# Fourth product of a fused attention and two-layer chain: a third pair of token tiles in seven block products, weights converted by contraction block

## The chip, the cores and the metric

The kernel runs on one core of one Trainium2 chip. The metric is the device time of one execution in microseconds (us). Engines are named as in the profile: PE is TensorE (matmuls), PEld its weight loads, ACT is ScalarE, DVE is VectorE, POOL is GpSimd, SP is SyncE, which issues the transfers here.

## The reference

```
attn = softmax(mask(q @ k^T / 8)) @ v            # 2 x 12 heads, 448 tokens, 64 wide
x    = attn as rows                               # 896 tokens x 768
h    = x @ moe_w_in;  g = h * sigmoid(h);  x = g @ moe_w_out      # 768 -> 2048 -> 768
h    = x @ w_in                                   # third product, 768 -> 1024
e    = exp(h - max(h));  solu = h * e / sum(e)
ln   = (solu - mean) / sqrt(var + 1e-6) * g_ln
out  = ln @ w_out                                 # fourth product, 1024 -> 768
```

The inputs are 64-bit floats in memory; the kernel converts the weights itself. Every product is made as three fp32r matmuls on a high and a low part of each operand (high x high, high x low, low x high).

## The kernel before, in words

The change touches the last two products. The 896 tokens are seven tiles of 128 (t = 0 to 6).

**Third product.** `gemm3(t)` makes 36 matmuls of 512 columns into a two-bank PSUM tile `h`; even tiles use the pool `psh0`, odd ones `psh1`, so tile t + 2 overwrites tile t. `chain(t)` takes the maximum on VectorE (L840, "reduce"), the exponential on ScalarE (L841, into the SBUF tile `e`) and, as the inner function `share`, the sums and the product on VectorE (L844 to L847). `scaled(t)` squares on ScalarE into `h` (L855, the last use of `h`), subtracts the mean from `e` (L856, ScalarE) and takes `rstd` from a small VectorE operation (L857) and a power on GpSimd (L858).

**Conversion of the fourth weight.** It comes in 16 chunks of 128 x 384 64-bit numbers. `feed4`, called through `fill` between the pieces of `chain`, works on a few of them at a time: ScalarE scales the upper words (`conv_a`, L259), VectorE puts the words together (`sign_low` L264, `shift_w` L276, `rest_high` L271), then `high4` (ScalarE, L772) and `low4` (VectorE, L777) give the high and low part of gain x weight. The 16 blocks are `b11`, `b21`, `b12`, `b22` (row half, column half), each of four contraction chunks k. Before, the chunks come block by block.

**Fourth product.** `turn(t)` transposes a tile: 16 small matmuls from `e` to the PSUM tile `tp`. Its tiles come from the list `turns`, first only `pst` (one buffer), later also `pstb`; each call takes the first pool of the list and moves it to the end. ScalarE and VectorE read `tp` into operands (high, L879; low, L883). One product is `product`: four k by three matmuls of 384 columns.

- `whole(t, n)` makes one column half of one tile in two products, four products a tile.
- `pair4(g)` makes tiles a = 2g + 1 and b = 2g + 2 together in seven products in place of eight, by seven sums of operands: "11", "12", "s4", "s2", "s3", "s1", "22" on the left with b11, b21, b22 and the sums of weights `t2`, `t3`, `t1`, `t4` on the right. `pre(g, n)`, n = 0 to 5, makes the left operands of a pair: n = 0 turns tile b, n = 1 turns tile a, n = 2 makes "s4", n = 3 to 5 make "s2", "s3", "s1", with a subtraction of 128 x 512 on GpSimd each.
- `sums4(k)` makes the sums of weights of chunk k (before: four scalings on ScalarE, L1020, four subtractions on GpSimd, L1022 to L1025); `split_t` splits them into high (ScalarE, L1030) and low (VectorE, L1031).

The order is written by hand. After every product `after()` runs the steps of a table, by number of the product. Before: tiles 0, 1 and 2 by `whole` (12 products), then `pair4(1)` and `pair4(2)` (14), 26 in all. The sums of weights are made at products 0 to 11. Engines work through their instructions in program order.

The output of a product lies in a PSUM bank of the pool `gm` (two buffers), for pairs in turn with `psq`, which lies where `psh0` was.

Of the kernel before, what the change touches and what calls it, by code (L numbers as in the profile page):

```python
# [8 lines left out]
F32 = mybir.dt.float32  # L9
F32R = mybir.dt.float32r  # L10
# [12 lines left out]
KD = DM // 128  # L23
# [63 lines left out]
def fused(ctx, tc, qk, vv, w1, w2, w3, w4, gl, out):  # L87
# [32 lines left out]
    with tc.manual_schedule():  # L120
# [153 lines left out]
        def shift_w(n, c):  # L274
            low = wraw[n, c][:, :, 0]
            nc.vector.tensor_scalar(low, low, 29, None, ALU.logical_shift_right)  # L276

        def top_bits(n, c):
            x = wx[n, c] = psw.tile([128, 512], F32, name="pw", tag="pw")[:, :CH]
            r = wraw[n, c]  # L280
            if n == 1 or n == 2 and c % 2 and c < HEAD + 4 * PARTS:
# [9 lines left out]
        def fresh(where):  # L291
            return where.tile([128, CH], F32, name="wx", tag="wx")
# [468 lines left out]
        aop[0, 1], aop[0, 2] = [pair_of(n, lambda m: spare[m]) for n in range(2)]  # L761

        def quad(m):
            n, k = divmod(m, KF2)
            return f"{k // K2 + 1}{n + 1}", k % K2, gain[:, k:k + 1]

        quads = {}

        def high4(m):
            z, k, g = quad(m)  # L770
# [2 lines left out]

        def low4(m):
            z, k, g = quad(m)
            h, l = split[4, z]
            nc.vector.scalar_tensor_tensor(l[:, k], quads[z, k], g, h[:, k].bitcast(F32), ALU.mult, ALU.subtract)  # L777
            ready.add((4, m))

        def feed4(between=lambda: None):  # L780
            m = fed[0]
            fed[0] += 1
            old = [order[pend.pop(0)][1] for _ in range(min(2, len(pend)) if len(pend) >= XS else min(1, len(pend)))]
            for c in old[:-1]:
                high4(c)
                low4(c)
            for c in old[-1:]:
                high4(c)
            if m < len(order):
                sign_low(*order[m], fresh(x4))  # L790
                if m + 1 < len(order):
                    shift_w(*order[m + 1])
                rest_high(*order[m])
                pend.append(m)
            between()
            for c in old[-1:]:
# [55 lines left out]
        def scaled(t):  # L852
            e, p3 = es4[t], hps[t].rearrange("p n (m q) -> p (n m) q", m=K2)
            col = lambda m: marks[t][:, m:m + 1]
            nc.scalar.activation(p3, e, AF.Square, bias=col(5), accum_out=col(6))  # L855
            nc.scalar.activation(e, e, AF.Identity, bias=col(5))  # L856
            nc.vector.tensor_scalar(col(7), col(6), 1.0 / DF2, 1e-6, ALU.mult, ALU.add)  # L857
            nc.gpsimd.tensor_tensor(col(9), col(7), mhalf, ALU.pow)  # L858
            rstd[t] = col(9)

# [120 lines left out]
        for t in range(NT):  # L981
            gemm3(t)
            if t == 0:
                fill()
            if t == NT - 2:
                turn(0)

            def first(between):
                if t == NT - 2:
                    take(0)  # L990
                fill(between)

            if t < NT - 1:
                chain(t, first, fill)
                scaled(t)
        areas = [token_rows(q, k)[:, :512] for q in "hl" for k in range(KD)] + spare[4:]
        places = {(1, 1): 0, (1, 2): 1, (2, 1): 2, (2, 2): 3}
        for g, at in ((1, (4, 5, 6, 7, 8, 9, None)), (2, (0, 1, 2, 3, None, 4, 5))):
            for z, n in zip(("11", "12", "s4", "s2", "s3", "s1", "22"), at):
                places[g, z] = n  # L1000
        for z, n in places.items():
            if n is not None:
                aop[z] = pair_of(n, lambda m: areas[m])
        aop[1, "22"], aop[2, "s3"] = aop[0, 1], aop[0, 2]

        def arrive(t):
            turn(t)
            take(t)

        arrive(1)  # L1010
        while pend:
            fill()
        w3p.release()
        t4p = pool("t4", side="right")
        for z in ("t2", "t3", "t1", "t4"):
            split[4, z] = [t4p.tile([128, K2, CH], F32R, name=f"{z}{p}", tag=f"{z}{p}") for p in "hl"]

        def sums4(k):
            for n, z in enumerate(QUADS):
                nc.scalar.activation(quads[z, k], quads[z, k], AF.Copy, scale=gain[:, k + K2 * (n // 2):k + K2 * (n // 2) + 1])  # L1020
            b11, b12, b21, b22 = [quads[z, k] for z in QUADS]
            nc.gpsimd.tensor_tensor(b11, b12, b11, ALU.subtract)  # L1022
            nc.gpsimd.tensor_tensor(b12, b12, b22, ALU.subtract)
            nc.gpsimd.tensor_tensor(b22, b22, b11, ALU.subtract)
            nc.gpsimd.tensor_tensor(b21, b21, b22, ALU.subtract)  # L1025

        def split_t(k):
            for z, q in (("t2", "22"), ("t3", "12"), ("t1", "11"), ("t4", "21")):
                h, l = split[4, z]
                nc.scalar.activation(h[:, k], quads[q, k], AF.Copy)  # L1030
                nc.vector.tensor_tensor(l[:, k], quads[q, k], h[:, k].bitcast(F32), ALU.subtract)  # L1031

        def pre(g, n):
            a, b = 2 * g + 1, 2 * g + 2
            s1, s3, s2, s4 = [rows(half(*at)) for at in ((b, 1), (b, 0), (a, 0), (a, 1))]
            if n == 0:
                turn(b)
# [22 lines left out]
        steps = {1: [lambda: sums4(1)], 2: [lambda: arrive(2)], 3: [lambda: split_t(0)], 4: [lambda: sums4(2)],  # L1060
                 5: [lambda: pre(1, 0)], 6: [lambda: sums4(3)], 7: [lambda: pre(1, 1)],
                 8: [lambda: scaled(NT - 1), lambda: split_t(1)], 9: [lambda: pre(1, 2)], 10: [lambda: split_t(2)],
                 11: [lambda: pre(1, 3), lambda: split_t(3)], 12: [lambda: pre(1, 4)], 13: [lambda: pre(1, 5)],
                 14: [lambda: pre(2, 0)], 15: [lambda: pre(2, 1)], 16: [lambda: pre(2, 2)],
                 17: [lambda: pre(2, 3), lambda: pre(2, 4)], 18: [lambda: pre(2, 5)]}
        at = iter(range(26))

        def after():
            for step in steps.get(next(at), ()):
                step()  # L1070

        sums4(0)
# [12 lines left out]
        turns[0].release()  # L1085
# [51 lines left out]
```

## Time and profile before

| what | value |
| --- | --- |
| median of 3 runs | 397.21 us (396.82 to 398.51) |
| profiled execution | 397.12 us |
| its span, first to last instruction | 395.2 us |
| PE busy | 387.5 us, 98% |
| DVE, ACT, POOL busy | 73%, 71%, 48% |
| mean granted TensorE clock | 1.000 |

Between the time of the profiled execution and its span lie 1.9 us that no engine shows. A time in a row counts from the start of the span. "x16" is the number of instructions that a row merges; the bracket at a row's end is the idle time before it and what ended it.

### The profile page before, as it was taken

The page shows a single profiled execution, that of the slowest core. Times are in us where ns is not written, and L with a number is a line of the kernel's source. Part 1 is how long each engine was busy: PE and PEld are TensorE (multiplying, and loading weights), DVE is VectorE, ACT ScalarE, POOL GpSimd, SP SyncE. Part 2 cuts the span into 40 slices and gives each one's busy share as a digit, 9 for nine tenths or more (in the row PEclk, how much of TensorE's full clock was granted, in tenths as well). Part 3 has the DMA queues.
Part 4 walks back from the last instruction along what each step waited for, and adds up shares of the span by engine and source line. Part 5 has one row for each costly group of instructions (what it writes and reads, how often), then busy time and mean ns, then how long its engine had stood idle before and what let it go on. Part 6 is the DMA issues. An engine that isn't in the chain of part 4 may idle for free.

```text
span 395.2 us, 8157 instructions
## 1 busy us (share of the span) xinstructions
PE 387.5 (98%) x2914; PEld 364.0 (92%) x2914; DVE 290.3 (73%) x681; ACT 279.7 (71%) x655; POOL 188.6 (48%) x236
## 2 busy tenths in 40 slices
PE   8799999999999999999999999999999999999996
PEld 5677888999999999999999999999988888999995
DVE  3999999477665755677566577776999996667943
ACT  5999998756474655775666787786767874998530
POOL 3898897324372563638566345554001000595450
PEclk9999999999999999999999999999999999999999
DMA  7964202244434343446343667787024310011121
GB/s 235 399 213 139 101 7 77 81 127 153 127 116 119 121 119 120 117 124 202 89 152 120 191 179 230 238 245 224 14 80 121 98 62 2 20 41 41 41 81 60
DMA packets 20152, 49.68 MB, mean 126 GB/s; under 512 B 2320, under 2 KB 4880, under 8 KB 20112
## 3 DMA queue, kind: packets, MB, share of 16 engines
q1 hardware_dynamic: 20112, 49.16, 39.7%
q8 instruction: 23, 0.38, 0.4%
q14 instruction: 17, 0.14, 0.1%
HBM read 46.40 MB, written 2.75 MB: 124 GB/s over the span
## 4 chain that ended last, share of the span: by engine, by line
PE 92%; DVE 4%; ACT 3%; issue 0%
PE h L397 8%; PE h L396 8%; PE h L395 8%; PE h L824 5%; PE h L825 5%; PE h L826 5%; PE ps L904 5%; PE h L555 4%; PE h L557 4%; PE h L556 4%; PE ps L906 4%; PE ps L905 4%; PE x L229 4%; PE x L164 3%; ACT e L175 3%; PE x L202 2%
## 5 line engine op out<-in xcount | busy, mean ns | idle before, releaser
L259 ACT ACTIVATE wr<-wr 128x384 f32<-128x384 f32 x92 | 54.3, 591 | 10.4 <-DMA wr<-w_in 10.2
L396 PE MATMUL h<-l,wh 128*128 128x448 f32 x174 | 61.3, 352 | 0.0
L395 PE MATMUL h<-h,wh 128*128 128x448 f32 x174 | 61.3, 352 | 0.0
L397 PE MATMUL h<-h,wl 128*128 128x448 f32 x174 | 61.3, 352 | 0.0
L289 DVE SCALAR_TENSOR_TENSOR pw<-wr,pw 128x384 uint32<-128x384 uint32 x78 | 43.5, 557 | 13.3 <-ACT pw L285 13.2
L188 POOL TENSOR_TENSOR e<-e,st 128x64 f32<-128x64 f32 (+6 forms) x76 | 45.5, 633 | 11.4 <-DVE st L170 6.9
L414 POOL TENSOR_TENSOR gl<-sg,gh 128x448 fp32r<-128x448 f32 x29 | 32.7, 1145 | 36.9 <-ACT sg L412 36.9
L175 ACT ACTIVATE e<-e,st 128x256 f32<-128x256 f32 (+6 forms) x84 | 41.8, 507 | 4.2 <-DVE st L170 4.1
L326 DVE TENSOR_TENSOR wl<-pw,wh 128x384 fp32r<-128x384 f32 x30 | 16.7, 557 | 32.5 <-ACT wh L322 31.8
L322 ACT ACTIVATE wh<-pw 128x384 fp32r<-128x384 f32 x30 | 14.8, 493 | 36.1 <-PE h L396 27.5
L170 DVE CUSTOM_DVE_ANT_0 e<-x,mask 128x448 f32<-128x448 f32 (+6 forms) x84 | 30.5, 414 | 5.4 <-PE x L164 5.4
L858 POOL TENSOR_TENSOR s<-s,mhalf 128x1 f32<-128x1 f32 x7 | 4.2, 594 | 61.3 <-DVE s L857 61.3
L326 POOL TENSOR_TENSOR wl<-wx,wh 128x384 fp32r<-128x384 f32 x21 | 21.2, 1008 | 25.5 <-ACT wh L322 25.4
L395 PEld LDWEIGHTS h<-h,wh 128*128 128x128 f32 x174 | 32.9, 189 | 0.1
L397 PEld LDWEIGHTS h<-h,wl 128*128 128x128 f32 x174 | 32.9, 189 | 0.0
L396 PEld LDWEIGHTS h<-l,wh 128*128 128x128 f32 x174 | 32.9, 189 | 0.0
L824 PE MATMUL h<-w3h,h 128*128 128x512 f32 x84 | 31.9, 380 | 0.0
L825 PE MATMUL h<-w3l,h 128*128 128x512 f32 x84 | 31.9, 379 | 0.0
L826 PE MATMUL h<-w3h,l 128*128 128x512 f32 x84 | 31.8, 379 | 0.0
L555 PE MATMUL h<-gh,wh 128*128 128x448 f32 x90 | 31.7, 352 | 0.0
L557 PE MATMUL h<-gh,wl 128*128 128x448 f32 x90 | 31.7, 352 | 0.0
L556 PE MATMUL h<-gl,wh 128*128 128x448 f32 x90 | 31.7, 352 | 0.0
(294 smaller groups left out, 1104.1 us busy)
## 6 DMA issues: line engine op xcount, KB each, us to landing
wr<-w_in SPq DMA_DIRECT2D x96, 384.0 KB, 3.2
qk<-qk_in SPq DMA_DIRECT2D x11, 448.0 KB, 5.5
v<-vv_in SPq DMA_DIRECT2D x12, 256.0 KB, 6.6
out<-o SPq DMA_DIRECT2D x14, 192.0 KB, 1.9
qk<-qk_in SPq DMA_DIRECT2D x2, 128.0 KB, 2.8
qk<-qk_in SPq DMA_DIRECT2D x1, 192.0 KB, 3.4
gain<-gl_in SPq DMA_DIRECT2D x1, 4.0 KB, 3.9
```

The source lines that it names most:

```text
L175: nc.scalar.activation(ep(p, u), ep(p, u), AF.Exp, bias=st[p % 4][:, u:u + 1], scale=-1.0, accum_out=st[p % 4][:, 8 + u:9 + u])
L188: eng.tensor_tensor(ep(p, u), ep(p, u), r.to_broadcast([128, wide(u)]), ALU.mult)
L259: nc.scalar.activation(high, high, AF.Copy, scale=DOWN)
L395: nc.tensor.matmul(ps[:, :S], wh, rh, start=turn == 0 and k % NB == 0, stop=False)
L396: nc.tensor.matmul(ps[:, :S], wh, rl, start=False, stop=False)
L397: nc.tensor.matmul(ps[:, :S], wl, rh, start=False, stop=turn == 1 and k % NB == NB - 1)
L555: nc.tensor.matmul(ps[:, :S], wh, rh, start=f == CF[0], stop=False)
L556: nc.tensor.matmul(ps[:, :S], wh, rl, start=False, stop=False)
L557: nc.tensor.matmul(ps[:, :S], wl, rh, start=False, stop=f == CF[-1])
L824: nc.tensor.matmul(ps[:, n], yh[k][:, at], wh, start=k == 0, stop=False)
L825: nc.tensor.matmul(ps[:, n], yh[k][:, at], wl, start=False, stop=False)
L826: nc.tensor.matmul(ps[:, n], yl[k][:, at], wh, start=False, stop=k == KD - 1)
```

## The change

- Tiles 1 and 2 become a third pair, `pair4(0)`, ahead of the others: four products of `whole` (tile 0) and three pairs of seven, 25 in all.
- The weight chunks come by contraction block: chunk m is now k = m // 4 of block 11, 21, 12, 22 in turn (also in the array's layout).
- From the fourth chunk on, VectorE writes the shifted low word into a `gm` PSUM tile (`top_bits`, L283), sets the sign there (`signed`, L290) and reads it from there (`rest_high`), in place of L276, L264 and a shift in SBUF.
- `low4` leaves VectorE: GpSimd multiplies the chunk by the gain (ScalarE for every fourth chunk, L786) and subtracts the high part (L789). After every fourth chunk GpSimd makes the sums of weights at once (`sums4`).
- `turn(2)` and `pre(0, 0)` stand behind the third product, `turn(1)` is in `pre(0, 1)` behind the first product of tile 0; the split of the sums goes sum by sum, in halves, at products 1 to 8. The power on GpSimd comes one tile later (`root`).

```
 def quad(m):
-    n, k = divmod(m, KF2)
-    return f"{k // K2 + 1}{n + 1}", k % K2, gain[:, k:k + 1]
+    k, n, z = m // 4, m // 2 % 2, m % 2
+    return f"{z + 1}{n + 1}", k, gain[:, k + K2 * z:k + K2 * z + 1]
...
 def low4(m):
     z, k, g = quad(m)
-    h, l = split[4, z]
-    nc.vector.scalar_tensor_tensor(l[:, k], quads[z, k], g, h[:, k].bitcast(F32), ALU.mult, ALU.subtract)
+    (h, l), x = split[4, z], quads[z, k]
+    if m % 4 == 3:
+        nc.scalar.activation(x, x, AF.Copy, scale=g)
+    else:
+        nc.gpsimd.tensor_tensor(x, x, g.to_broadcast([128, CH]), ALU.mult)
+    nc.gpsimd.tensor_tensor(l[:, k], x, h[:, k].bitcast(F32), ALU.subtract)
     ready.add((4, m))
+    if m % 4 == 3:
+        sums4(k)
...
-                sign_low(*order[m], fresh(x4))
+                early = order[m] in wx
+                if early:
+                    signed(*order[m])
+                else:
+                    sign_low(*order[m], fresh(x4))
                 if m + 1 < len(order):
-                    shift_w(*order[m + 1])
-                rest_high(*order[m])
+                    top_bits(*order[m + 1])
+                rest_high(*order[m], fresh(x4) if early else None)
...
+            def second():
+                for _ in range((1, 1, 2, 1, 1, 0)[t]):
+                    fill()
...
-        arrive(1)
         while pend:
             fill()
+        turn(2)
+        pre(0, 0)
+        root(NT - 2)
...
-        steps = {1: [lambda: sums4(1)], 2: [lambda: arrive(2)], 3: [lambda: split_t(0)], 4: [lambda: sums4(2)],
-                 5: [lambda: pre(1, 0)], 6: [lambda: sums4(3)], 7: [lambda: pre(1, 1)],
...
+        for n, g, m in ((0, 0, 1), (1, 0, 2), (3, 0, 3), (4, 0, 4), (5, 0, 5), (8, 1, 0), (9, 1, 1), (10, 1, 2), (11, 1, 3),
+                        (12, 1, 4), (13, 1, 5), (14, 2, 0), (15, 2, 1), (16, 2, 2), (17, 2, 3), (17, 2, 4), (18, 2, 5)):
+            steps.setdefault(n, []).append(lambda g=g, m=m: pre(g, m))
+        steps[0] += [lambda: scaled(NT - 1), lambda: spread(NT - 1)]
+        steps[13].append(lambda: root(NT - 1))
+        for n, z in enumerate(("t2", "t3", "t1", "t4")):
+            for i, ks in enumerate((range(2), range(2, K2))):
+                steps.setdefault(2 * n + i + 1, []).append(lambda z=z, ks=ks: split_t(z, ks))
...
-        for t in (1, 2):
-            for n in range(2):
-                whole(t, n)
...
-        for g in (1, 2):
+        for g in range(3):
             pair4(g)
```

**ScalarE around the end of the third product.** The first row is the square of tile 5, the last the exponential of tile 6; `d_3800` and `h_4282` are operands read from `tp`. Before:

```order
L855 ACTIVATE h,s<-e,s 128x1024
L856 ACTIVATE e<-e,s 128x1024
L879 ACTIVATE h_4282<-tp 128x512
L879 ACTIVATE h_4284<-tp 128x512
L772 ACTIVATE b22h<-wx,gain 128x384 x2
L1020 ACTIVATE wx<-wx,gain 128x384 x4
L841 ACTIVATE e,s<-h,s 128x1024
```

With the change:

```order
L873 ACTIVATE h,s<-e,s 128x1024
L874 ACTIVATE e<-e,s 128x1024
L780 ACTIVATE b12h<-wx,gain 128x384
L780 ACTIVATE b22h<-wx,gain 128x384
L786 ACTIVATE wx<-wx,gain 128x384
L1011 ACTIVATE e<-tp 128x512
L903 ACTIVATE d_3800<-tp 128x512
L859 ACTIVATE e,s<-h,s 128x1024
```

The two reads of `tp` moved behind the conversions of the last two chunks; before, tile 1's reads stood ahead of them.

**VectorE at the same place, with the change.** The first row belongs to `scaled(5)`, the last is the maximum of tile 6.

```order
L878 TENSOR_SCALAR s<-s 128x1
L916 TENSOR_TENSOR e<-tp,e 128x512
L907 TENSOR_TENSOR d_3801<-tp,d_3800 128x512
L858 TENSOR_REDUCE s<-h 128x1
```

The add and the low part of tile 2's second half (operand "22") now stand between them; before, the low parts of tile 1 (two rows L883) and of the last chunks (two rows L777) stood there.

**VectorE in the first pair's products.** `t1l` and `t4l` are low parts of weight sums, `o<-ps,s,o` takes a product out of PSUM, `l_4326<-tp` and `e<-tp` belong to the next pair's `pre`. With the change:

```order
L963 SCALAR_TENSOR_TENSOR o<-ps,s,o 128x384
L1079 TENSOR_TENSOR t1l<-wx,t1h 128x384 x2
L963 SCALAR_TENSOR_TENSOR o<-ps,s,o 128x384
L1079 TENSOR_TENSOR t1l<-wx,t1h 128x384 x2
L963 SCALAR_TENSOR_TENSOR o<-ps,s,o 128x384 x2
L1079 TENSOR_TENSOR t4l<-wx,t4h 128x384 x2
L963 SCALAR_TENSOR_TENSOR o<-ps,s,o 128x384
L916 TENSOR_TENSOR e<-tp,e 128x512
L907 TENSOR_TENSOR l_4326<-tp,l_4325 128x512
L1079 TENSOR_TENSOR t4l<-wx,t4h 128x384 x2
L963 SCALAR_TENSOR_TENSOR o<-ps,s,o 128x384 x2
L907 TENSOR_TENSOR l_4328<-tp,l_4327 128x512
```

Before, where the first pair's products begin:

```order
L1031 TENSOR_TENSOR t2l<-wx,t2h 128x384
L1031 TENSOR_TENSOR t3l<-wx,t3h 128x384
L1031 TENSOR_TENSOR t1l<-wx,t1h 128x384
L1031 TENSOR_TENSOR t4l<-wx,t4h 128x384
L939 SCALAR_TENSOR_TENSOR o<-ps,s,o 128x384 x2
L892 TENSOR_TENSOR e<-tp,e 128x512
```

All low parts of the sums stood ahead of the first sum taken out of PSUM; now they stand among the first pair's sums, the last two behind the next pair's `pre(1, 0)`.

## Rows read from the trace of the kernel before

**Rows 1.** The page, part 1: busy time of each engine.
```profile
PE 387.5 (98%) x2914; PEld 364.0 (92%) x2914; DVE 290.3 (73%) x681; ACT 279.7 (71%) x655; POOL 188.6 (48%) x236
```

**Rows 2.** Windows, third and fourth product: PE, PEld, DVE, ACT, POOL busy; clock, DMA.
```profile
280.20:335.60 55.40, 55.40 (x270) 47.88 (x268) 49.66 (x107) 38.16 (x66) 2.75 (x5) 1.00 0.22 65
335.60:391.50 55.90, 55.85 (x409) 53.98 (x408) 37.03 (x64) 36.49 (x72) 28.76 (x26) 1.00 0.12 43
```

**Rows 3.** Waits from 280 us on: us in total, times, longest.
```profile
ACT e L841 <- DVE s L840: 12.3, 7, 3.4
...
PEld tp L874 <- issue: 1.8, 7, 0.3
```

**Rows 4.** Timeline of PE, fourth product: start, length, instruction.
```profile
335.64 0.71 PE L874 MATMUL tp<-ident,e 64*128 64x64 f32 x16
336.28 0.43 PE L904 MATMUL ps<-b11h,d 128*128 128x384 f32 x1
...
338.34 0.33 PE L904 MATMUL ps<-b21h,d 128*128 128x384 f32 x1
...
387.39 0.33 PE L904 MATMUL ps<-t1h,l 128*128 128x384 f32 x1
...
389.34 0.33 PE L904 MATMUL ps<-t4h,l 128*128 128x384 f32 x1
```

**Rows 5.** Timeline of VectorE, last tiles of the third product.
```profile
327.14 1.23 DVE L840 TENSOR_REDUCE s<-h 128x1 f32<-128x1024 f32 x1 [0.66 <-PE h L826]
330.61 1.29 DVE L883 TENSOR_TENSOR d<-tp,d 128x512 fp32r<-128x512 f32 x2 [2.25 <-ACT d L879]
...
332.42 0.45 DVE L276 TENSOR_SCALAR wr<-wr 128x384 uint32<-128x384 uint32 x1
...
335.08 0.15 DVE L847 TENSOR_SCALAR s<-s 128x1 f32<-128x1 f32 x1
...
340.96 1.22 DVE L840 TENSOR_REDUCE s<-h 128x1 f32<-128x1024 f32 x1
...
345.17 0.15 DVE L847 TENSOR_SCALAR s<-s 128x1 f32<-128x1 f32 x1
```

**Rows 6.** Timeline of ScalarE, same place.
```profile
335.27 1.12 ACT L855 ACTIVATE h<-e,s 128x1024 f32<-128x1024 f32 x1 [3.08 <-DVE s L847]
...
336.54 1.15 ACT L856 ACTIVATE e<-e,s 128x1024 f32<-128x1024 f32 x1
337.60 1.07 ACT L879 ACTIVATE h<-tp 128x512 fp32r<-128x512 f32 x2
...
339.56 2.13 ACT L1020 ACTIVATE wx<-wx,gain 128x384 f32<-128x384 f32 x4
...
347.23 0.53 ACT L1030 ACTIVATE t2h<-wx 128x384 fp32r<-128x384 f32 x1
```

**Rows 7.** Timelines of VectorE and GpSimd, two places where both work.
```profile
262.05 1.01 POOL L326 TENSOR_TENSOR wl<-wx,wh 128x384 fp32r<-128x384 f32 x1 [2.31 <-ACT wh L322]
262.43 0.56 DVE L289 SCALAR_TENSOR_TENSOR pw<-wr,pw 128x384 uint32<-128x384 uint32 x1
...
365.33 0.55 DVE L1031 TENSOR_TENSOR t4l<-wx,t4h 128x384 fp32r<-128x384 f32 x1
365.41 1.61 POOL L883 TENSOR_TENSOR d<-e,d 128x512 fp32r<-128x512 f32 x1 [1.36 <-ACT d L879]
365.80 1.64 DVE L1031 TENSOR_TENSOR t2l<-wx,t2h 128x384 fp32r<-128x384 f32 x1
```

**Rows 8.** Timeline of VectorE: two reads of tp, two sums out of PSUM.
```profile
338.70 1.29 DVE L883 TENSOR_TENSOR h<-tp,h 128x512 fp32r<-128x512 f32 x2 [1.23 <-ACT h L879]
...
368.77 1.13 DVE L939 SCALAR_TENSOR_TENSOR o<-ps,s,o 128x384 f32<-128x384 f32 x2
```

**Rows 9.** Groups of GpSimd's instructions: count, busy us, mean ns, idle.
```profile
L188 POOL TENSOR_TENSOR e<-e,st 128x384 f32<-128x384 f32 x11 | 9.2, 835 | 1.4 <-DVE st L181 1.4
...
L883 POOL TENSOR_TENSOR l<-e,l 128x512 fp32r<-128x512 f32 x2 | 2.6, 1276 | 0.0
```

More of the change, by code (lines that the diff above doesn't have):

```diff
@@ L278, in top_bits @@
         def top_bits(n, c):
-            x = wx[n, c] = psw.tile([128, 512], F32, name="pw", tag="pw")[:, :CH]
+            late = (n, c) >= (4, XS)
+            x = wx[n, c] = (gm if late else psw).tile([128, 512], F32, name="pw", tag="gm" if late else "pw")[:, :CH]
             r = wraw[n, c]
-            if n == 1 or n == 2 and c % 2 and c < HEAD + 4 * PARTS:
+            if n == 1 or late or n == 2 and c % 2 and c < HEAD + 4 * PARTS:
                 nc.vector.tensor_scalar(x.bitcast(U32), r[:, :, 0], 29, None, ALU.logical_shift_right)
@@ L763, in quad, with sums4 @@
         def quad(m):
-            n, k = divmod(m, KF2)
-            return f"{k // K2 + 1}{n + 1}", k % K2, gain[:, k:k + 1]
+            k, n, z = m // 4, m // 2 % 2, m % 2
+            return f"{z + 1}{n + 1}", k, gain[:, k + K2 * z:k + K2 * z + 1]
         quads = {}
+        def sums4(k):
+            b11, b12, b21, b22 = [quads[z, k] for z in QUADS]
+            nc.gpsimd.tensor_tensor(b11, b12, b11, ALU.subtract)
+            nc.gpsimd.tensor_tensor(b12, b12, b22, ALU.subtract)
+            nc.gpsimd.tensor_tensor(b22, b22, b11, ALU.subtract)
+            nc.gpsimd.tensor_tensor(b21, b21, b22, ALU.subtract)
         def high4(m):
@@ L856, in scaled, with spread, root @@
             nc.scalar.activation(e, e, AF.Identity, bias=col(5))
+        def spread(t):
+            col = lambda m: marks[t][:, m:m + 1]
             nc.vector.tensor_scalar(col(7), col(6), 1.0 / DF2, 1e-6, ALU.mult, ALU.add)
+        def root(t):
+            col = lambda m: marks[t][:, m:m + 1]
             nc.gpsimd.tensor_tensor(col(9), col(7), mhalf, ALU.pow)
@@ L979, in fill @@
                 between()
[L981 to L1008, printed above, removed]
-        arrive(1)
[L1011 to L1031, printed above, removed]
         def pre(g, n):
@@ L1036, in pre @@
             if n == 0:
-                turn(b)
+                if g:
+                    turn(b)
                 nc.scalar.activation(s3, tps[b, 1], AF.Copy)
@@ L1058, in pre @@
                 low((g, z), x, nc.gpsimd)
-        steps = {1: [lambda: sums4(1)], 2: [lambda: arrive(2)], 3: [lambda: split_t(0)], 4: [lambda: sums4(2)],
-                 5: [lambda: pre(1, 0)], 6: [lambda: sums4(3)], 7: [lambda: pre(1, 1)],
[L1062 to L1065, printed above, removed]
@@ L1066, in fused, with first @@
-        at = iter(range(26))
+        for n, z in enumerate(("22", "11", "12", "s4")):
+            aop[0, z] = pair_of(n + 2, lambda m: spare[m])
+        for t in range(NT):
+            gemm3(t)
+            if t == 0:
+                fill()
+            if t == NT - 1:
+                break
+            if t == NT - 2:
+                turn(0)
+            def first(between):
+                if t == NT - 2:
+                    take(0)
+                fill(between)
+            def second():
+                for _ in range((1, 1, 2, 1, 1, 0)[t]):
+                    fill()
+            chain(t, first, second)
+            scaled(t)
+            spread(t)
+            if t:
+                root(t - 1)
@@ new lines, in fused @@
+        areas = [token_rows(q, k)[:, :512] for q in "hl" for k in range(KD)] + spare
+        for g, at in ((0, {"s2": 0, "s3": 1, "s1": 2}),
+                      (1, {"22": 3, "11": 4, "12": 5, "s4": 6, "s2": 7, "s3": 9, "s1": 10}),
+                      (2, {"22": 11, "11": 0, "12": 1, "s4": 2, "s2": 8, "s3": 4, "s1": 5})):
+            for z, n in at.items():
+                aop[g, z] = pair_of(n, lambda m: areas[m])
+        while pend:
+            fill()
+        turn(2)
+        pre(0, 0)
@@ new lines, in fused, with split_t @@
+        root(NT - 2)
+        w3p.release()
+        t4p = pool("t4", side="right")
+        for z in ("t2", "t3", "t1", "t4"):
+            split[4, z] = [t4p.tile([128, K2, CH], F32R, name=f"{z}{p}", tag=f"{z}{p}") for p in "hl"]
+        def split_t(z, ks):
+            (h, l), q = split[4, z], {"t2": "22", "t3": "12", "t1": "11", "t4": "21"}[z]
+            for k in ks:
+                nc.scalar.activation(h[:, k], quads[q, k], AF.Copy)
+                nc.vector.tensor_tensor(l[:, k], quads[q, k], h[:, k].bitcast(F32), ALU.subtract)
@@ new lines, in fused @@
+        steps = {}
+        for n, g, m in ((0, 0, 1), (1, 0, 2), (3, 0, 3), (4, 0, 4), (5, 0, 5), (8, 1, 0), (9, 1, 1), (10, 1, 2), (11, 1, 3),
[6 more added lines that the diff above has]
+                steps.setdefault(2 * n + i + 1, []).append(lambda z=z, ks=ks: split_t(z, ks))
@@ L1068, in after @@
+        at = iter(range(25))
         def after():
@@ L1070, in after @@
                 step()
-        sums4(0)
         psh.pop().release()
@@ L1123 @@
         "w3": chunks(parted(inputs["moe2_w_in"].reshape(KD, 128, 2, 512)).transpose(1, 2, 0, 3)),
-        "w4": chunks(parted(inputs["moe2_w_out"].reshape(KF2, 128, 2, CH)).transpose(1, 2, 0, 3)),
+        "w4": chunks(parted(inputs["moe2_w_out"].reshape(2, K2, 128, 2, CH)).transpose(2, 1, 3, 0, 4)),
         "gl": inputs["moe2_g_ln"].reshape(KF2, 128).T,
```

## Prediction

> **What bounds the kernel now.** I read the page first: TensorE is busy 387.5 of 395.2 us [rows 1]. As busy matmuls need not be matmuls at full pace, I went on to the windows of the two stages that the change touches: TensorE is busy in all but 0.05 us of both, at the full clock (1.00), and no other engine is full over a whole stage; GpSimd works 2.75 of 55.4 us in the third product [rows 2]. The waits say that nothing there waits on another engine for TensorE's sake: what TensorE shows is 1.8 us of "issue" in seven turns, while ScalarE waits 12.3 us for maxima [rows 3]. Last the timeline, for the pace: a product starts every 389.34 - 387.39 = 1.95 us, twelve matmuls of 0.1625; a turn takes 336.28 - 335.64 = 0.64 and makes the product behind it 0.11 longer (338.34 - 336.28 = 2.06) [rows 4]. So TensorE's sequence is the time, without a gap. Less of it is a gain of just that; any wait put into it is a loss of just that. The question is whether the other engines, which had slack, still have it when the first pair begins after 4 products in place of 12.
>
> **Removed.** One product, 26 to 25: -1.95 us. Turns and third product keep their count. This is 0.49% of 397.12, so even undisturbed the change is at the edge of the 0.5% which a measurement of this kernel can tell from none.
>
> **Costs nothing, and why.** Converting a chunk on VectorE by way of PSUM takes three steps of about 0.56, the row of the same form [rows 7], and the low part goes. That lightens VectorE, and hides under TensorE's 55 us; nothing there was waited for. GpSimd gets 12 multiplications (0.84, the broadcast row of the same size), 16 subtractions and 16 for the sums (1.01): 10.1 + 16.2 + 16.2 = 42.5 us, from about 287 to 345, some 58 us; up to 335.6 it was idle there but for 2.75 [rows 2, 7, 9]. If GpSimd could not keep up, products 0 to 3 would wait for low parts. ScalarE gets four scalings earlier and loses 16 later.
>
> **First wait: turn 1.** `turns` holds `pst` when tile 2 is turned; `pstb` is added behind it, so the next call takes `pst` again. Tile 1's turn, behind product 0, thus has to wait until tile 2 has been read out of it, and the last reader is VectorE's low part of "22". When is that?
> - VectorE's maximum of tile 5 starts at 327.14 after idling for TensorE [rows 5], so lighter conversion cannot bring it forward. The `share` of tile 5 ended at 335.08 + 0.15 = 335.23; one L276 less ahead of it (0.45) gives 334.8.
> - ScalarE then: square 336.54 - 335.27 = 1.27, subtraction 337.60 - 336.54 = 1.06, three scaled copies of 0.51 (2.13 for four, 0.60 the last) = 1.53, two reads of `tp` 1.07 [rows 6]: 339.7. The last chunks' conversions now stand ahead of the reads.
> - VectorE's first read of a turned tile starts after ScalarE's second (330.61, released by ACT) [rows 5]; add and low take 1.29 [rows 8]: 341.0.
> Product 0 ends at 338.34 as tile 0's first did [rows 4]. TensorE waits **2.7 us**. Behind the turn stand all products. VectorE's maximum of tile 6, queued behind the low part, starts at about 340.95, just where it did (340.96), so `share(6)` ends at 345.3 again [rows 5].
>
> **Second wait: the low parts of t4, in product 10.** From 345.3 VectorE has five operations of 128 x 512 at 0.60 (two in 1.29) and a small one, 3.1 [rows 8]: 348.4. ScalarE then makes the high part of "s4" and the first `t2h` (0.53 each) [rows 6]: VectorE starts the 16 low parts at 349.6. Up to the last of t4 it has 16 x 0.47 (365.80 - 365.33), five sums out of PSUM at 0.57 (two in 1.13), and the add and low of the next pair, 1.2 [rows 7, 8]: 7.5 + 2.8 + 1.2 = 11.5. While it does that, GpSimd makes four subtractions of 1.28 [rows 9]. Such a pair of operations, each with two operands in SBUF, does not overlap: `t2l` at 365.80 took 1.64 where its neighbour took 0.55, while GpSimd's subtraction (365.41, 1.61) ran; an operation with one operand in PSUM kept its 0.56 at 262.43 beside GpSimd's [rows 7]. Each of the four can cost 0 to 1.1, so 0 to 4.4; I take 4, because the 16 stand close together and each subtraction falls among them. Last low part: 349.6 + 11.5 + 4 = 365.1.
> The Trainium skill (SBUF — State Buffer, Who interferes with whom) says that a VectorE instruction with two SBUF inputs and a GpSimd instruction that reads SBUF exclude each other, and that the later one blocks for the whole instruction. By that rule alone four full subtractions would count, about 5.1 us, and the sum below would come to 403.8; the row at 365.80 agrees in kind, with 1.1.
> TensorE, released at 341.0: turn 0.64, product 1 in 2.06, seven of 1.95, turn 0.64, product 9 in 2.06, turn 0.64: product 10 at 360.7. It needs the last low part at its eleventh matmul, 0.11 + 1.63 later: 362.4. Wait: **2.7 us** (it may begin in products 8 and 9, same sum). If ScalarE's copies between the halves starve VectorE of some 2 us (an estimate: ScalarE's own queue there has 16 high parts, 4 copies and 4 operands, 24 x 0.5 = 12 against VectorE's 11.5, each waiting for the other in turn), the last low part is at 363.1 without any port wait, and 367.5 with all of it.
>
> **Third wait: the left operands of pair 1.** Behind the last low part VectorE has two sums (1.1) and then the low part of "11" (0.69): +1.8, where product 11 wants it with its third matmul, +0.65. That is 1.1. The low part of "12" comes 0.6 + 1.2 + 0.57 later, 2.4 against a product of 1.95: 0.4. "s4" follows with add 0.6, ScalarE 0.65 and GpSimd 1.28, 2.5 against 1.95: 0.6. Together **2.1 us**. Afterwards operands are ahead; pair 2 has its turns before products 15 and 16, first use at 18, and should not wait.
>
> **Sum.** 2.7 + 2.7 + 2.1 - 1.95 = +5.55 on the profiled 397.12: **402.7 us**. The median of the runs (397.21) is 0.09 from it, which I leave out.
>
> **Rivals.**
> - *Ports don't collide.* The four subtractions fall into VectorE's pauses. Last low part at 363.1 (ScalarE-fed): second wait 0.7, sum 2.7 + 0.7 + 2.1 - 1.95: 400.7. At 361.0, with no pause, second and most of the third wait go: 2.7 + 0.6 - 1.95: 398.5. For it: a sum out of PSUM does not collide. Against: 365.80.
> - *Both add.* 367.5: second wait 5.1, 405.1.
> - *GpSimd falls behind.* Its chain for the last chunk starts at 337.8 and must give b12's and b22's low parts by about 343; if each operation cost a third more, 42.5 would be 57 of 58 us, and every us lost there is one of TensorE's: some 405 or more. Against: rows of 0.84 and 1.01 beside a busy VectorE whose other operand is in PSUM [rows 7, 9].
> - *Not slower.* VectorE, lighter by some 0.7 us a chunk, runs ahead, the tile is read out by 338.3 and the low parts of t4 are there by 359.7 (362.4 less the first wait): 397.12 - 1.95 = 395.2, no change by our bound. It decides at the first wait: `share(5)` would have to end before 332.1. Against: the maximum of tile 5 waits for TensorE at 327.14, and what follows it is a chain across ScalarE.
>
> **How the numbers follow.** My forecast (401.3 to 404.0) 0.60; no collision 0.20, most of it above 400; both add 0.08; GpSimd behind 0.03; not slower 0.09. The range 400.0 to 404.5 leaves out the last two, a little of the second and the end of the third: 0.60 + 0.17 + 0.03 = 0.80 stays. Slower 0.91 (all but the last); same 0.07; faster 0.02, since 395.2 is not beyond the bound.
>
> **What would show it.** In the changed profile: the second turn of the fourth product idle for 2 to 3 us, released by VectorE's low part of tile 2; gaps in the products with t3, t1, t4 of the first pair, released by VectorE's split; single gaps of half to one us in 11, 12, s4 of the next pair; none in the last pair, and none in the third product; `t2l` to `t4l` rows of over 1.2 us beside GpSimd's. Wrong it is if the turn starts at 338.4, or if VectorE's split is done before 362.

## The result, and the profile after

The changed kernel takes 402.84 us (median of 4 runs, 402.35 to 402.88) against 397.5 us (4 runs, 396.82 to 398.51): a ratio of 1.0129, 95% interval 1.0105 to 1.0153. The forecast was slower, 402.7 us. The profiled execution took 402.79 us with a span of 401.0 us, against 397.12 and 395.2.

The page's part 1 of the changed kernel, which answers to [rows 1]; then two windows, from the third product's first matmul to tile 2's turn and from there to the last matmul, which answer to [rows 2]; then all that TensorE itself waited for behind the third product:

```profile
PE 388.2 (97%) x2902; PEld 363.4 (91%) x2902; DVE 291.3 (73%) x676; ACT 276.0 (69%) x645; POOL 219.2 (55%) x268
```
```profile
280.10:336.23 56.13, 55.85 (x269) 47.70 (x269) 47.47 (x96) 40.65 (x69) 38.41 (x42) 1.00 0.21 64
336.23:397.60 61.37, 56.67 (x397) 53.62 (x396) 40.20 (x69) 30.21 (x59) 23.59 (x21) 0.97 0.11 39
```
```profile
PE tp L898 <- DVE d L907: 3.0, 1, 3.0
PE ps L930 <- DVE l L907: 0.7, 1, 0.7
PE ps L930 <- POOL d L907: 0.4, 1, 0.4
PE ps L929 <- DVE t4l L1079: 0.4, 1, 0.4
```

Read the windows first: TensorE, which had no gap [rows 2], now idles 0.3 us in the third product and 4.7 behind it, where the clock is no longer 1.00 on average. The timeline of TensorE shows the places:

```profile
280.10 0.38 PE L842 MATMUL h<-w3h,h 128*128 128x512 f32 x1
...
296.11 0.48 PE L842 MATMUL h<-w3h,h 128*128 128x512 f32 x1 [0.28 <-ACT h L873]
...
335.92 0.38 PE L844 MATMUL h<-w3h,l 128*128 128x512 f32 x1
...
338.76 0.33 PE L930 MATMUL ps<-b11h,d 128*128 128x384 f32 x1
342.12 0.71 PE L898 MATMUL tp<-ident,e 64*128 64x64 f32 x16 [3.04 <-DVE d L907]
...
344.29 0.52 PE L929 MATMUL ps<-b21l,d 128*128 128x384 f32 x1
344.61 0.52 PE L930 MATMUL ps<-b21h,d 128*128 128x384 f32 x1
...
365.47 0.43 PE L929 MATMUL ps<-t4l,d 128*128 128x384 f32 x1 [0.39 <-DVE t4l L1079]
367.59 0.43 PE L930 MATMUL ps<-b11h,l 128*128 128x384 f32 x1 [0.71 <-DVE l L907]
...
372.53 0.43 PE L930 MATMUL ps<-b22h,d 128*128 128x384 f32 x1 [0.40 <-POOL d L907]
...
397.22 0.33 PE L930 MATMUL ps<-t4h,d 128*128 128x384 f32 x1
```

A 128x384 matmul follows the one before by 0.1625 where nothing waits [rows 4]; at 344.29 and 344.61 it is 0.32. The windows of that stretch give the granted clock (the third number from the end):

```profile
344.00:346.00 2.00, 2.00 (x8) 2.00 (x7) 1.55 (x4) 1.32 (x4) 1.92 (x3) 0.50 0.00 0
346.00:348.00 2.00, 2.00 (x11) 2.00 (x10) 1.97 (x7) 1.69 (x3) 0.17 (x1) 0.72 0.00 0
```

Last, VectorE's and GpSimd's timelines, where the low parts of the t operands are made:

```profile
350.06 1.29 POOL L907 TENSOR_TENSOR d<-e,d 128x512 fp32r<-128x512 f32 x1 [3.89 <-ACT d L903]
352.70 1.60 POOL L907 TENSOR_TENSOR h<-e,h 128x512 fp32r<-128x512 f32 x1 [1.36 <-ACT h L903]
354.99 2.91 POOL L907 TENSOR_TENSOR h<-e,h 128x512 fp32r<-128x512 f32 x2 [0.68 <-ACT h L903]
```
```profile
350.50 2.67 DVE L1079 TENSOR_TENSOR t2l<-wx,t2h 128x384 fp32r<-128x384 f32 x4 [1.18 <-ACT t2h L1078]
353.09 2.10 DVE L1079 TENSOR_TENSOR t3l<-wx,t3h 128x384 fp32r<-128x384 f32 x2
355.35 2.96 DVE L1079 TENSOR_TENSOR t3l<-wx,t3h 128x384 fp32r<-128x384 f32 x2 [0.17 <-ACT t3h L1078]
...
358.76 1.01 DVE L1079 TENSOR_TENSOR t1l<-wx,t1h 128x384 fp32r<-128x384 f32 x2
...
364.87 1.01 DVE L1079 TENSOR_TENSOR t4l<-wx,t4h 128x384 fp32r<-128x384 f32 x2
...
369.17 0.68 DVE L907 TENSOR_TENSOR l<-tp,l 128x512 fp32r<-128x512 f32 x1
```

Two low parts take 1.01 (t1l, t4l) when GpSimd is idle; beside its subtractions t3l's take 2.10 and 2.96. From 350.50 to the last row VectorE pauses once, for 0.17 us.

**Where the time went.** In the kernel before, the first and the last matmul of the third product and the last matmul of all stood here:

```profile
280.29 0.38 PE L824 MATMUL h<-w3h,h 128*128 128x512 f32 x1
...
335.33 0.38 PE L826 MATMUL h<-w3h,l 128*128 128x512 f32 x1
...
391.13 0.33 PE L906 MATMUL ps<-t4h,l 128*128 128x384 f32 x1
```

From the third product's first matmul (280.10) to the last one of all (397.22) it is 117.12 us; before it was 391.13 - 280.29 = 110.84. This stretch is called the length below. Of the +6.28: the third product +0.78 (335.92 - 280.10 = 55.82 between its first and last matmul, 335.33 - 280.29 = 55.04 before); turn 1 +3.1 (it starts 342.12 - 338.76 = 3.36 behind the matmul ahead of it, where the kernel before took 342.33 - 342.08 = 0.25); the low clock +1.7 (its two products, 3.12 and 2.57 from start to start, for 2.06 and 1.95); t4 +0.65 and the next pair's first three products +0.98, +0.37, +0.67 (start to start, so that the 0.1 with which TensorE starts again is in them); the removed product -1.95; together +6.3. The time of the profiled executions grew by less, 402.79 - 397.12 = 5.67, as the third product began 0.19 earlier, what follows the last matmul was 0.29 shorter in the span, and 0.13 lies outside the span. Lengths are compared below, since the third product's first matmul stood between 279.86 and 281.50 in the runs, though no edit touches what comes ahead of it.

### The profile page after: what moved, and what is told of

Read it like the earlier page. It is cut to its first block, busy times and chain, and to the rows that moved or that the text cites. A ratio compares the mean times of both kernels' runs of the same rounds, so it can differ in the third digit from the quotient of the medians.

```text
span 401.0 us, 8178 instructions
## 1 busy us (share of the span) xinstructions
PE 388.2 (97%) x2902; PEld 363.4 (91%) x2902; DVE 291.3 (73%) x676; ACT 276.0 (69%) x645; POOL 219.2 (55%) x268
## 4 chain that ended last, share of the span: by engine, by line
PE 76%; DVE 7%; ACT 6%; issue 6%; POOL 4%; DMA 1%; SPq 0%; POOLq 0%; ACTq 0%; DVEq 0%
PE h L398 8%; PE h L397 8%; PE h L396 8%; PE x L229 4%; PE h L556 4%; PE h L558 4%; PE h L557 4%; PE x L164 3%; PE h L842 3%; ACT e L175 3%; PE h L844 3%; PE h L843 3%; PE x L202 3%; PE ps L930 2%; PE ps L928 2%
## 5 line engine op out<-in xcount | busy, mean ns | idle before, releaser
L290 DVE SCALAR_TENSOR_TENSOR pw<-wr,pw 128x384 uint32<-128x384 uint32 x90 | 51.6, 573 | 12.8 <-ACT pw L286 12.6
L283 DVE TENSOR_SCALAR pw<-wr 128x384 uint32<-128x384 uint32 x46 | 26.9, 586 | 0.3 <-DMA wr<-w_in 0.3
```

The lines of the kernel that those rows point to most:

```text
L290: nc.vector.scalar_tensor_tensor(x, wraw[n, c][:, :, 1], 0x80000000, x, ALU.bitwise_and, ALU.bitwise_or)
```

## Experiments

The theory: **(A)** one queue, VectorE's, sets the date of all behind it, and TensorE's waits only show where it meets that queue. The rival **(B)**: each wait has a price of its own, and whatever removes one gains its length. Each recorded expectation names an A and a B of its own, with figures for that run; "A's range" below means those figures.

**Turn 1 into the other PSUM pool.**
```diff
-        turns.append(pool("pstb", 1, space=PS))
+        turns.insert(0, pool("pstb", 1, space=PS))
```


> The list of PSUM pools is turned round, so that tile 1 is turned into the second pool and does not wait for tile 2 to be read out. Theory A (one chain from tile 6's share over VectorE's queue sets how soon the first pair can run, so waits change places): the 3.0 to 3.2 us before the turn of tile 1 and the fall of the clock behind it go, but about 2 us come back at the next use of that pool, in products 4 to 6, and 1 to 2 more at t3 and t4; time 401.5 to 403. Theory B (each wait stands alone): the changed kernel's 402.8 less 3.1 of wait and 1.6 of low clock, 398.1, with the waits at t4 and at the next pair no larger than before (0.5 and 1.5).


403.44 us (1.0150, 1.0129 to 1.0171). The 3.0 us wait and the low clock are gone, and the end is where it was: 398.37 - 281.23 = 117.14. The longest of TensorE's waits, same view as above:
```profile
PE ps L928 <- ACT h L873: 1.7, 1, 1.7
PE ps L929 <- DVE t4l L1079: 1.4, 1, 1.4
PE ps L930 <- DVE l L907: 0.7, 1, 0.7
```
B falls: 4.8 us were removed from that place and not 0.1 gained; waits of about the same sum stand elsewhere. The time is 0.4 above A's range (401.5 to 403).

**t4's low parts on GpSimd.**
```diff
-                nc.vector.tensor_tensor(l[:, k], quads[q, k], h[:, k].bitcast(F32), ALU.subtract)
+                (nc.gpsimd if z == "t4" else nc.vector).tensor_tensor(l[:, k], quads[q, k], h[:, k].bitcast(F32), ALU.subtract)
```


> Only t4's four low parts of each half move from VectorE to GpSimd, which idles for 13 us behind its subtractions. Theory A (VectorE's queue of 16 low parts and five sums is late at t4 and at the next pair's left operands): the wait at t4 (0.5) and most of the 1.5 at the next pair go, the 3.1 before the turn of tile 1 and the low clock behind it stay: 400.8 to 401.5. Theory B (GpSimd's larger subtractions collide with VectorE's at the SBUF port, so work put on GpSimd comes back as longer VectorE operations): no gain, 402.5 to 403.5, with the t1 and t2 rows still above 2 us.


403.99 us (1.0165, 1.0146 to 1.0184); length 117.33. What A expected did not come; B's "no gain" did, 0.5 above its range. I first put it down to a longer stretch of low clock in this run (0.50 up to 348, 0.64 in the two us behind). That was wrong: two of its four runs had a mean clock of 1.00 and were no faster (403.63 and 405.0, against 403.88 and 404.11 with 0.992). **Both edits together** tell better:

> The turned list of pools and t4's low parts on GpSimd together. Each alone left the end where it was: the one moved the first wait to the fifth product and to t4, the other one's gain went into a longer stretch at the low clock. Theory A (two limits stand behind one another, ScalarE's queue up to the square of tile 6 and VectorE's queue of low parts; each hides the other): together 1.5 to 2.5 us less between the third product's first matmul and the last one than in the changed kernel (117.1): 114.6 to 115.7, time 401 to 402; the wait of 1.9 at the fifth product and one of 0.3 to 0.6 at t3 stay. Theory B (the end is set by something common to both, the left operands of the next pair): 117 again, with more wait at the next pair.


404.05 us (1.0166, 1.0147 to 1.0185), length 118.12: both figures missed. VectorE and GpSimd:
```profile
358.76 2.28 POOL L1079 TENSOR_TENSOR t4l<-wx,t4h 128x384 fp32r<-128x384 f32 x2 [0.51 <-ACT t4h L1078]
```
```profile
359.11 2.34 DVE L1079 TENSOR_TENSOR t1l<-wx,t1h 128x384 fp32r<-128x384 f32 x2
```
VectorE's two low parts of t1 went from 1.01 to 2.34 beside GpSimd's two of t4: what VectorE is spared it loses again. In the run with t4's edit alone the first of these rows took 2.40.

**Tile 6 ahead of tile 2.** Reduction, exponential and `share` of tile 6 go ahead of `turn(2)` and `pre(0, 0)`.
```diff
+        share6 = chain(NT - 1, None, None)
         while pend:
             fill()
+        share6()
         turn(2)
         pre(0, 0)
...
-        chain(NT - 1, lambda between: between(), lambda: whole(0, 0))
+        whole(0, 0)
```


> The maximum, exponential and share of tile 6 go ahead of the reading out of tile 2 in every queue. Theory A (tile 6's chain over VectorE and ScalarE is the start of all that is late): turn of tile 1 waits longer, by the share's some 4 us if VectorE takes it first, but t4 and the next pair no longer wait; 402 to 405, with the wait in one place. Theory B (the order of the two does not matter as both use the same VectorE time): 402.8 within 0.5, with the waits where they were.


404.0 us (1.0162, 1.0141 to 1.0183), length 117.68. The wait before turn 1 grew to 4.4 us and t4 no longer waits; the next pair still does (0.5 and 0.4). As A expected are the time, the longer wait at the turn (by 1.4 us, not 4) and none at t4; that the next pair would not wait was missed.

**Words shifted in SBUF again.**
```diff
-                    top_bits(*order[m + 1])
+                    shift_w(*order[m + 1])
```


> The late chunks' words are shifted in SBUF on VectorE, as in the kernel before, instead of by way of PSUM; all else of the change stays. Theory A (a VectorE operation with two SBUF inputs and a GpSimd one hold each other up, and GpSimd now works through the whole third product): VectorE's steps of 0.56 become 0.8 to 1.2 there, the third product shows gaps of 1 to 5 us in all where it has 0.8, time 404 to 408. Theory B (VectorE has slack enough in the third product and PSUM only changes where the words lie): 402.8 within 0.7.


405.17 us (1.0228, 1.0168 to 1.0288), length 118.73. Windows of the third product, the changed kernel and then this run (DVE is the fourth number behind the window, POOL the sixth):
```profile
312.00:328.00 16.00, 16.00 (x84) 13.79 (x86) 13.53 (x29) 13.25 (x20) 12.77 (x16) 1.00 0.22 70
```
```profile
312.00:328.00 16.00, 15.99 (x74) 13.37 (x73) 15.79 (x30) 12.01 (x20) 15.61 (x12) 1.00 0.25 74
```
Both engines grow by over 2 us in 16, with 30 VectorE operations for 29 and 12 of GpSimd for 16. Rows of this run, VectorE's shift in SBUF (L276) and a multiplication on GpSimd:
```profile
315.81 1.29 DVE L276 TENSOR_SCALAR wr<-wr 128x384 uint32<-128x384 uint32 x1
...
324.20 0.45 DVE L276 TENSOR_SCALAR wr<-wr 128x384 uint32<-128x384 uint32 x1
```
```profile
323.77 2.14 POOL L788 TENSOR_TENSOR wx<-wx,gain 128x384 f32<-128x384 f32 x1
```
Where the shift took 0.45, GpSimd's multiplication beside it took 2.14 in place of 0.83; at 315.81 and again at 320.05 the shift itself took 1.29 and 1.28. So an operation with a single input in SBUF was part of it too. The route by way of PSUM is what lets the two engines work side by side: its three steps take 0.57 to 0.74 in the changed kernel, in the same window. It is worth 1.6 us here, within A's range: 0.7 in the third product (335.92 - 280.10 = 55.82 grew to 56.53) and 0.9 at turn 1 (a wait of 3.94 for 3.04).

**The conversions alone.** Tiles 1 and 2 are turned and multiplied whole, 26 products, operands placed as in the kernel before.
```diff
-        turn(2)
-        pre(0, 0)
+        arrive(1)
...
+        for t in (1, 2):
+            for n in range(2):
+                whole(t, n)
...
-        for g in range(3):
+        for g in (1, 2):
```


> The change's conversions alone (chunks by contraction block by way of PSUM, low parts and sums on GpSimd during the third product); tiles 1 and 2 are turned and multiplied whole as in the kernel before, 26 products. Theory A (the loss sits in the early first pair): the third product keeps the 0.6 to 0.9 us of gaps that it has in the changed kernel, there is no wait of 2 us or more behind it, and first matmul of the third product to last matmul is 111.0 to 112.0 against 110.8 before: 397.5 to 398.7. Theory B (the conversions themselves bring the loss: their work on GpSimd and ScalarE in the third product): 400 or more, with waits at the first products.


397.7 us (1.0011, 1.0000 to 1.0022), length 393.11 - 281.50 = 111.61. That is +0.77 on before, and it is the third product's alone (55.82 here too). The rest of the loss belongs to the early first pair.

**The first pair's low parts on VectorE.**
```diff
-                low((g, "s4"), s4, nc.gpsimd)
+                low((g, "s4"), s4, nc.gpsimd if g else nc.vector)
...
-                low((g, z), x, nc.gpsimd)
+                low((g, z), x, nc.gpsimd if g else nc.vector)
```


> The four low parts of the first pair's sums move from GpSimd (1.3 us each) to VectorE (some 0.6 each); nothing else of the changed kernel is touched, so GpSimd is idle while VectorE makes the low parts of the t operands. Theory A (what VectorE loses there is the exclusion of two engines that both read two SBUF operands): t2's and t3's eight low parts, 7.7 us in the changed kernel, go back to 8 x 0.47 = 3.8, the four new operations cost 2.5, VectorE's last low part of t4 comes 1.2 to 1.6 earlier, and the end with it by up to that: 115.7 to 116.8 from the third product's first matmul to the last one (117.1). Theory B (the long rows are VectorE waiting for ScalarE's high parts, booked as busy): the rows stay long, the added 2.5 us come on top, 118.5 to 120.


402.03 us (1.0129, 1.0106 to 1.0152), length 115.99. Though VectorE has four operations more, its low parts are done earlier:
```profile
350.46 1.96 DVE L1079 TENSOR_TENSOR t2l<-wx,t2h 128x384 fp32r<-128x384 f32 x4
...
353.12 1.02 DVE L1079 TENSOR_TENSOR t3l<-wx,t3h 128x384 fp32r<-128x384 f32 x2
...
355.39 1.02 DVE L1079 TENSOR_TENSOR t3l<-wx,t3h 128x384 fp32r<-128x384 f32 x2
...
367.88 0.68 DVE L907 TENSOR_TENSOR l<-tp,l 128x512 fp32r<-128x512 f32 x1
```
t2 and t3 take 1.96 + 2.04 = 4.00 for 2.67 + 5.06 = 7.73: the four subtractions cost VectorE 3.7 us. The wait before turn 1 is as long as in the changed kernel (2.99), this time at a clock of 1.00.

**What all these runs have in common.** From timelines: the first matmul of the third product, the start of VectorE's low part of half 12 (the operand "12") of the next pair (the `l<-tp,l` row last shown), the start of the last matmul.
```
run                       first    low 12    last     length   last - low 12
changed kernel            280.10   369.17   397.22   117.12   28.05
other pool                281.23   370.33   398.37   117.14   28.04
t4's low on GpSimd        281.00   370.29   398.33   117.33   28.04
both                      280.43   370.51   398.55   118.12   28.04
tile 6 first              280.18   369.82   397.86   117.68   28.04
words in SBUF             280.50   371.19   399.23   118.73   28.04
pair 0 low on VectorE     279.93   367.88   395.92   115.99   28.04
all edits (below)         280.01   366.42   394.46   114.45   28.04
no overlap (below)        280.04   362.81   390.86   110.82   28.05
```
In nine kernels with a wait at turn 1 of 0 to 4.4 us, with and without the low clock, the last matmul comes 28.04 or 28.05 us behind that one operation. The end is the date at which VectorE has worked off its queue up to it. This shows A, with the place named: TensorE's last waits hang on that operation. VectorE's pauses between the first low part of t2 and it are 0.2 to 1.7 us in these kernels, all for ScalarE's high parts, so ScalarE, which feeds the queue, has that much of a share in the date. The later runs move the operation itself and stand outside the table.

**All edits at once:** turned list of pools, t4's low parts on GpSimd, tile 6 first and its square right behind, all chunks but the last multiplied on GpSimd, the next pair's first two steps earlier.
```diff
-            if m % 4 == 3:
+            if m == N4 - 1:
                 nc.scalar.activation(x, x, AF.Copy, scale=g)
...
+        scaled(NT - 1)
+        spread(NT - 1)
         root(NT - 2)
...
-        steps[0] += [lambda: scaled(NT - 1), lambda: spread(NT - 1)]
+        steps[2].append(lambda: centred(NT - 1))
```


> Turned list of pools, t4's low parts on GpSimd, tile 6's maximum to share ahead of the reading out of tile 2, its square right behind that, the multiplication of all chunks but the last on GpSimd, the next pair's first operands a step earlier. Theory A (all the loss is queue order on ScalarE and VectorE, none of it total work): the waits before the products fall to 1.5 us or less in all and the removed product shows: 109.5 to 111.5 from the third product's first matmul to the last one, against 110.8 before and 117.1 in the changed kernel; time 396 to 398. Theory B (VectorE and ScalarE have too much work between the third product and the second pair, whatever its order): 113 to 116, time 399.5 to 402, VectorE busy over nine tenths up to the last low part.


400.5 us (1.0083, 1.0066 to 1.0101), length 114.45: in B's range. The third product's gaps are gone (335.09 - 280.01 = 55.08), so they came of the multiplications that stood on ScalarE ahead of the square; the other edits act behind them. But t2's, t3's and t1's low parts still run beside GpSimd's (2.82, 1.79, 2.89 and 2.10 where 1.96 and 1.02 would do).

**No overlap.** On top of that, the first pair's four low parts and t4's last two blocks on VectorE; t4's first two blocks split by ScalarE and GpSimd, and t2's high parts made, where these engines idled; the centring of tiles 5 and 6 (the subtraction of the mean on ScalarE) later.
```diff
+        high_t("t4", range(2))
+        low_t("t4", range(2), nc.gpsimd)
         share6 = chain(NT - 1, None, None)
...
-                low((g, z), x, nc.gpsimd)
+                low((g, z), x, nc.gpsimd if g else nc.vector)
```


> As the run with all edits, and now no GpSimd subtraction stands beside VectorE's low parts: the first pair's four on VectorE, t4's first two blocks split by ScalarE and GpSimd before the low part of tile 2 (GpSimd idles 5.8 us there), t2's high parts ahead of the s4 high part on ScalarE, tile 5's centring later. Theory A (in that run 4.8 us of its VectorE time were collisions and 2.5 waits for ScalarE, and VectorE's queue sets the end): the waits of 4.6 us in all fall to 0 to 1.5, 109.8 to 111.5 from the third product's first matmul to the last one against 110.8 before; time 396 to 397.8. Theory B (VectorE's work itself is too much by then): 112.5 to 115 and VectorE without a pause from the reading out of tile 2 to the next pair.


396.72 us (0.9985, 0.9973 to 0.9997), length 110.82. Of 4.6 us of waits (from start to start) 1.7 stay, all at the next pair: length and time are in A's range, the waits a little above their bound of 1.5. **Half 12 earlier:**
```diff
                 low((g, "11"), tps[a, 1], nc.vector)
+                low((g, "12"), tps[a, 2], nc.vector)
```
(and `pre(1, 2)` at step 8 in place of 10.)


> The run without overlap, with the low part of half 12 straight behind that of 11 and the next pair's s4 begun two products earlier. Theory A (VectorE's queue order is all that is left): the two last waits (1.14 at the next pair's 21 product and 0.57 at its 22) fall to under 0.4 together; 109.1 to 109.6 from the third product's first matmul to the last one against 110.8 before, which is the removed product less 0.2 to 0.8; time 395.0 to 396.0. Theory B (VectorE has no slack there, and what is moved forward pushes the sums out of PSUM back until TensorE lacks a bank): 110.5 or more, with waits released by VectorE's sums.


396.52 us (0.9990, 0.9981 to 0.9999), length 110.82 again: A missed. The length is in B's range, but not by B's way, since no wait was released by VectorE's sums: the two waits gave way to two at s2, one product on:
```profile
366.59 0.43 PE L934 MATMUL ps<-t2h,d 128*128 128x384 f32 x1 [0.27 <-ACT d L909]
367.94 0.43 PE L936 MATMUL ps<-t2h,d 128*128 128x384 f32 x1 [0.76 <-POOL d L913]
```
The high part of s2 stood behind 2.17 us of centring on ScalarE, which had idled 5.22 us just before. The reverse of one edit on this kernel, **the first pair's low parts back on GpSimd** (the `low` lines as in the changed kernel):
```diff
-                low((g, z), x, nc.gpsimd if g else nc.vector)
+                low((g, z), x, nc.gpsimd)
```

> As the run with half 12 early, with the first pair's four low parts back on GpSimd (1.3 us each) instead of VectorE (0.6 each). Theory A (each of the four costs VectorE, by exclusion, more than the operation that it saves): VectorE's t2 and t3 rows grow by 3 to 4.5, its own work shrinks by 2.5, waits of 0.7 to 2 us appear at t1 or at the next pair: 0.5 to 2 us more than that run. Theory B (the load that GpSimd takes is a gain and the long rows were something else): equal or up to 1 us faster.


398.03 us (1.0028, 1.0018 to 1.0038), length 392.31 - 279.86 = 112.45, +1.63 on the same length without it, as A expected. The rows of t2 and t3 take 7.17 where they took 4.08 without it. VectorE:
```profile
346.13 4.13 DVE L1084 TENSOR_TENSOR t2l<-wx,t2h 128x384 fp32r<-128x384 f32 x4
350.19 3.04 DVE L1084 TENSOR_TENSOR t3l<-wx,t3h 128x384 fp32r<-128x384 f32 x4
```
**Centring into the idle stretch**, `pre(1, 3)` at step 8:
```diff
-(8, pre, 1, 1), (8, pre, 1, 2), (9, centred, NT - 2), (9, centred, NT - 1)):
+(8, pre, 1, 1), (8, centred, NT - 2), (8, centred, NT - 1),
+                               (8, pre, 1, 2), (8, pre, 1, 3)):
```


> As the run with half 12 early; the centring of tiles 5 and 6 moves into ScalarE's idle 5.2 us ahead of the next pair's s4, and the s2 part of that pair is begun three products earlier, so that its high part no longer stands behind 2.2 us of centring and two copies. Theory A (ScalarE's queue order is what is left): the last waits (1.6 us) fall under 0.4, 109.0 to 109.5 from the third product's first matmul to the last one against 110.8 before; 394.8 to 395.7, a gain of 0.3 to 0.5 per cent over the kernel before. Theory B (the wait moves one product on again, as it did from 1.7 to 1.6 in the step before): 110.3 to 110.9 and a wait at s3 or s1 of the next pair.


395.15 us (0.9944, 0.9928 to 0.9960): faster than both kernels, in A's range. One gap of 0.27 is left in the fourth product. Its length is 389.61 - 280.35 = 109.26, 1.58 below before: the removed product less that gap and its restart.

## Why the prediction was right

The sign, the time (402.7 for 402.84, range 400.0 to 404.5) and the mechanism held: TensorE waits, and most of it hangs on VectorE's queue. The second wait did not have the predicted size, and two losses were in no term.

- **Removed product, -1.95:** right; the last run has it back nearly whole.
- **Costs nothing:** right behind the third product, but not in it. The conversions alone cost 0.78 there, where the prediction named "none in the third product" as a sign. The step that failed is "ScalarE gets four scalings earlier": I counted its work and not what stands behind it. The copy that multiplies every fourth chunk came ahead of the square of a tile, for which a PSUM bank waits. GpSimd kept up (from 292 us on multiplications 0.83, low parts and sums 0.99 to 1.02). VectorE's three steps by way of PSUM, taken at 0.56, took 0.57 to 0.74 between 312 and 328 us.
- **First wait, 2.7:** 3.04 by the row, at the place and with the releaser forecast. Counted as the prediction counts, from the end of product 0 (338.76 + 0.16), it is 3.2.
- **Second wait, 2.7:** mis-sized, 0.65. It fell on the eighth matmul of product 10, which needs the first of t4's last two low parts, not on the eleventh. Its VectorE side was close: the last low part of t4 forecast for 365.1, measured 364.87 + 1.01 = 365.88. The collisions were taken at 4 and measured 3.7. TensorE, though, came to product 10 at 363.68 in place of 360.7: 0.6 by the third product (tile 2's turn at 336.23 for 335.64), 0.5 by the first wait and 1.7 by the low clock, which the prediction did not have at all. Of the signs named, the gaps at t3 and t1 and the long rows of t1l and t4l did not come: GpSimd's four subtractions were over at 354.99 + 2.91 = 357.90, ahead of both. Since the queue sets the date, what delays TensorE alone ahead of it is so much less of this wait.
- **Third wait, 1.1 + 0.4 + 0.6 = 2.1:** 0.98 + 0.37 + 0.67 = 2.02.
- **The rule of the Trainium skill** (SBUF — State Buffer, Who interferes with whom) asked, as the prediction estimated from it, for 5.1 us of collision where I took 4, of 4.4 at most by my row. The runs agree with it in kind in both directions (taken out, put back, put beside t1). Operations with one input in PSUM kept nearly their pace, or the words in SBUF would not have cost 1.6; but two SBUF inputs, as the prediction put it, are not the whole of it, since L276 with one of them was slowed, or slowed GpSimd, as well. The size was 3.7. By the rows that is 0.7 for the first subtraction, which was under way for 0.44 when VectorE's low parts began, and about 1.0 to 1.1 for each of the other three, where GpSimd's own rows grew too (1.60, and 2.91 for two, where one takes 1.29 undisturbed).
- **The rivals:** "not slower" named the wrong place. It does not decide at the first wait, which can be removed for nothing (117.14), but at the end of VectorE's queue.

So the sum is better than its parts: what I called second and third wait is a date, and the first wait lies ahead of it. Adding them gave about that date, since I worked the second out as the rest against TensorE's own, and so what the second wait lacked (2.05) was made up by the low clock and the third product, which I had at nothing (1.7 and 0.78). That the total came within 0.2 us was luck in part: the length grew by 6.28 where the sum has 5.55, and the profiled time only by 5.67.

## What to carry over

Before pricing waits one by one, find the last operation of the other engine's queue that TensorE needs: if that queue has no pause, waits ahead of it are worth nothing and only its work and order count. Work moved to an idle GpSimd is not free: beside VectorE's subtractions of two SBUF operands it cost VectorE 3.7 us for the 2.4 that it saved (four of 0.6), and it belongs into stretches where VectorE reads PSUM or idles. A stage that gives up products early needs its operands early; count the engine time between the two dates, not the share of busy time over the stage (VectorE: 73% on the page).

## What the hardware showed unexpectedly

TensorE had full clock (1.00) through the third product, idled 3.0 us before turn 1, and from 343.96 to 346.85 its ten matmuls stood 0.32 apart in place of 0.1625; the granted clock was 0.50, the level of 1.2 GHz, then 1.00 again. In four of the five profiled runs with a wait of 2.99 to 4.4 us at that place the clock fell so; in the profiled run with pair 0's low parts on VectorE, after 2.99 us, it stayed at 1.00. Two further runs of that same kernel had mean clocks of 0.990 and 0.996, so one and the same kernel did both; after the 1.75 us at the fifth product in the profiled runs "other pool" and "both" it stayed at 1.00. What tells these apart is open. Here it cost nothing at the end, as the table shows; where TensorE sets the time it would, by these rows, cost 1.7 us beyond the wait.
